# A decode attention block with its gradients: hand order on every engine, and weight-group transfers issued from GpSimd

## The chip, the cores and the metric

One core of a Trainium2 chip. The metric is device time in microseconds (us) of one execution, the median of the runs of a kernel. A "tile" is one head's K or V block, 128 partitions by 16 KB (2 MB).

## The reference

The forward pass of one decode step (layer norm, attention of one query over a cache of 8,192 positions in 32 heads, and a gated MLP in parallel) and the gradients of all its inputs except one constant:

```python
def _A_ref(x, k_cache, v_cache, wq, wo):       # Hq = Hkv = 32, Sk = 8192, Dh = 128, D = 640
    q = (x @ wq).reshape(B, Sq, Hq, Dh).transpose(0, 2, 1, 3)
    scores = jnp.einsum("bhqd,bhkd->bhqk", q, k) * (Dh ** -0.5)
    p = softmax(scores)
    o = jnp.einsum("bhqk,bhkd->bhqd", p, v)
    return o.transpose(0, 2, 1, 3).reshape(B, Sq, Hq * Dh) @ wo
def _B_ref(x, w1, w3, w2):                     # F = 1728
    return (silu(x @ w1) * (x @ w3)) @ w2
xn = layernorm(A_x)
out = A_x + _A_ref(xn, A_k_cache, A_v_cache, A_wq, A_wo) + _B_ref(xn, B_w1, B_w3, B_w2)
# returned: out, and its gradients for A_x, A_k_cache, A_v_cache, A_wq, A_wo, B_w1, B_w3, B_w2
```

The gradient of each K and V tile is an outer product as large as the tile. So the kernel reads about 152 MB and writes about 151 MB, and nearly all of it is 32 K and 32 V tiles in and 64 gradient tiles out.

## The kernel before

Ten tile slots hold K and V; a gradient overwrites its tile in place, is stored, and the slot takes the next load. All large transfers go through one in-order queue, SyncE's. Four heads form a group that shares a piece of `wq` and `wo`.

```python
    def fifo(out_, in_):
        tc.keep_in_program_order(nc.sync.dma_start(out_, in_))
    def load_group(g):                       # [cut: tile allocation]
        fifo(wq_g[:], wq_v[:, :, g * GW:(g + 1) * GW])
        fifo(wo_g[:], wo_v[:, g * GH:(g + 1) * GH, :])
    def load_next():
        if not pending or len(free_slots) < lag[0]:     # lag is 2 in the steady state
            return
        kind, h = pending.pop(0)
        if kind == "K" and h % GH == GH - 1 and h // GH + 1 < NG:
            load_group(h // GH + 1)
        t = free_slots.pop(0)
        fifo(t[:], (kc if kind == "K" else vc)[h])
    def store(kind, h):                      # [cut: bookkeeping]
        fifo((dkc if kind == "K" else dvc)[h], t[:])
        free_slots.append(t)
        load_next()
    # [cut]
    def finish_group(g):                     # [cut: small products]
        for hh in range(GH):
            nc.vector.tensor_scalar(wo_g[:, hh, :], g_bc[:], od[:, hh, 0:1], None, ALU.mult)
        fifo(dwo_v[:, g * GH:(g + 1) * GH, :], wo_g[:])
        for ci in range(NC):
            # [cut] wq_g becomes its gradient
        fifo(dwq_v[:, :, g * GW:(g + 1) * GW], wq_g[:])
    # [cut]
    for h in range(H):
        if hh == GH - 1 and g + 1 < NG:
            prep_group(g + 1)
        sums(h)                              # 64 + 64 matmuls: o and dq
        outer_v(h, 0, J // 2)
        outer_v(h, J // 2, J)
        store("V", h)
        if h == 1:
            mlp()
        if h + 1 < H:
            rows(h + 1)
            dots_k(h + 1)                    # transposes and products with q
        outer_k(h, 0, J // 2)
        if h + 1 < H:
            probs(h + 1)
        outer_k(h, J // 2, J)
        store("K", h)
        if h + 1 < H:
            dots_v(h + 1)
        if hh == GH - 1:
            finish_group(g)
```

A lag of 2 means that a load is issued only when two slots are on the free list. It goes into the slot freed one store earlier, so that it need not wait for the store that was issued just before it.

## Time and profile before

| | before |
|---|---|
| median time | 758.96 us (3 runs, 758.43 to 759.77) |
| bytes moved | 304.62 MB, mean 402 GB/s |
| TensorE busy | 79% |
| VectorE busy | 59% |
| ScalarE busy | 44% |

The largest wait of TensorE in the kernel before (us in total, times, longest us). No K or V load is among its waits anywhere in the list:

```profile
PE hb L352 <- DVE U L349: 41.0, 24, 2.7
```

The largest wait of SyncE's DMA queue in the same kernel is for stores to land:

```profile
SPq L99 <- DMA out_dram<-kv: 448.9, 55, 14.7
```

The timeline of TensorE around one head (start, us, operation, count, and the idle time before it) shows the hole that the change wants to fill, 1.67 us before the dq sums:

```profile
503.43 2.12 PE L347 MATMUL hb<-P,kv 128*128 128x64 bf16 x64
...
507.21 2.11 PE L352 MATMUL hb<-U,kv 128*128 128x64 bf16 x64 [1.67 <-DVE U L349]
```

The end of the kernel before, in a table of stretches of 4 us (stretch, length, busy time and count of PE, PEld, DVE, ACT, POOL, granted clock, DMA share, GB/s):

```profile
744.00:748.00 4.00, 0.00 (x0) 0.00 (x0) 0.00 (x0) 0.00 (x0) 0.00 (x0) 0.50 0.97 383
748.00:752.00 4.00, 0.00 (x0) 0.00 (x0) 0.00 (x0) 0.00 (x0) 0.00 (x0) 0.50 0.53 186
752.00:756.00 4.00, 0.00 (x0) 0.00 (x0) 0.00 (x0) 0.00 (x0) 0.00 (x0) 0.50 0.06 20
```

A share of 0.06 is 1/16: one packet in flight. The end is a drain of stores.

### The profile page before, as it was taken

The numbers are of one execution on the slowest core, as the hardware profiler recorded it, in microseconds if no ns is written. First come the engines' busy times: TensorE is split into PE (matmuls) and PEld (weight loads), VectorE is DVE, ScalarE is ACT, GpSimd is POOL, SyncE is SP. The second block draws the span as 40 slices with busy tenths as digits, with TensorE's granted clock in tenths as the row PEclk, the third lists the DMA queues.
The fourth block names the chain that finished last, engine by engine and source line by source line (L and its number), as shares of the span: only waits on it lengthen the run. The fifth ranks groups of instructions, "written<-read, shape, count | busy, mean of one in ns | idle before, by whom it ended". The sixth has DMA issues, their size and how long they took to land. (4 is left out here: it accounts for less than half of the span.)

```text
span 756.8 us, 25031 instructions
## 1 busy us (share of the span) xinstructions
PE 601.0 (79%) x11263; PEld 561.1 (74%) x11263; DVE 447.1 (59%) x771; ACT 330.7 (44%) x668; POOL 0.7 (0%) x6
## 2 busy tenths in 40 slices
PE   2988798888898888888898889888898889888820
PEld 2887688887788778877787778777787778777710
DVE  4369658654566557654666557654666557654470
ACT  1632354454454444444554445444554445444500
POOL 0000000000000000000000000000000000000000
PEclk9998999999998999999998999999998999999965
DMA  8999999999999999999999999999999999999996
GB/s 332 389 420 413 401 418 410 416 427 403 426 424 388 416 396 428 421 426 381 403 427 368 400 404 401 429 420 413 359 429 409 360 416 383 427 425 420 391 418 263
DMA packets 44031, 304.62 MB, mean 402 GB/s; under 512 B 2836, under 2 KB 24980, under 8 KB 27540
## 3 DMA queue, kind: packets, MB, share of 16 engines
q1 hardware_dynamic: 43616, 302.69, 98.3%
q8 instruction: 88, 1.44, 0.7%
q10 hardware_dynamic: 308, 0.33, 0.2%
q14 instruction: 19, 0.16, 0.1%
HBM read 151.67 MB, written 151.34 MB: 400 GB/s over the span
## 5 line engine op out<-in xcount | busy, mean ns | idle before, releaser
L269 ACT COPY KT<-pT 128x512 f32<-128x512 f32 x512 | 289.9, 588 | 120.7 <-PE pT L267 74.1
L267 PE MATMUL pT<-ident_f,kv 128*128 128x128 f32 x2048 | 317.5, 287 | 0.1
L267 PEld LDWEIGHTS pT<-ident_f,kv 128*128 128x128 f32 x2048 | 230.4, 147 | 0.5 <-ACT kv L483 0.4
L278 PEld LDWEIGHTS <-KT 128*128 128x128 bf16 x4096 | 176.6, 99 | 30.8 <-ACT KT L269 21.5
L328 DVE TENSOR_TENSOR kv<-qd,P 128x4096 bf16<-128x4096 bf16 x64 | 145.7, 2286 | 25.4 <-PE hb L347 25.4
L328 DVE TENSOR_TENSOR kv<-qd,U 128x4096 bf16<-128x4096 bf16 x64 | 143.6, 2284 | 0.0
L352 PE MATMUL hb<-U,kv 128*128 128x64 bf16 x2048 | 74.8, 199 | 42.1 <-DVE U L349 41.0
L352 PEld LDWEIGHTS <-kv 128*128 128x128 bf16 x2048 | 73.4, 102 | 45.3 <-issue 45.1
L278 PE MATMUL sA<-cz,KT 128*128 128x64 bf16 x2048 | 99.3, 193 | 7.2 <-ACT KT L269 6.5
L278 PE MATMUL dA<-cz,KT 128*128 128x64 bf16 x2048 | 99.3, 194 | 6.4 <-ACT KT L269 6.3
L343 DVE SCALAR_TENSOR_TENSOR U<-dA,P 128x64 bf16<-128x64 f32 x32 | 7.4, 230 | 132.6 <-PE dA L278 132.6
L354 ACT COPY od_g<-hb 128x2 f32<-128x2 f32 x32 | 5.1, 160 | 152.3 <-DVE kv L328 93.7
L347 PE MATMUL hb<-P,kv 128*128 128x64 bf16 x2048 | 67.7, 192 | 0.0
L347 PEld LDWEIGHTS <-kv 128*128 128x128 bf16 x2048 | 67.3, 98 | 0.0
L236 DVE SCALAR_TENSOR_TENSOR KT<-wo_g,g_bc 128x640 bf16<-128x640 bf16 x32 | 26.3, 823 | 28.5 <-PE dA L278 28.0
L308 PEld LDWEIGHTS sA<-rsum,pm_one 128*128 128x128 f32 x64 | 9.5, 187 | 29.0 <-ACT E L307 29.0
L308 PE MATMUL sA<-rsum,pm_one 128*128 128x1 f32 x64 | 12.2, 260 | 22.6 <-ACT E L307 22.1
L307 ACT ACTIVATE E<-sA,negM 128x64 f32<-128x64 f32 x32 | 10.1, 314 | 44.2 <-DVE negM L304 44.1
L292 ACT CAST qd<-pT 128x256 bf16<-128x256 f32 x32 | 12.1, 377 | 39.0 <-PE pT L289 39.0
L391 DVE SCALAR_TENSOR_TENSOR wq_g<-wq_g,KT 128x512 bf16<-128x512 bf16 x40 | 26.3, 687 | 3.7 <-ACT KT L382 3.7
L300 DVE TENSOR_REDUCE mrow<-sA 128x1 f32<-128x64 f32 x32 | 7.1, 222 | 35.8 <-PE sA L278 35.3
L315 DVE RECIPROCAL rZ<-sA 128x1 f32<-128x1 f32 x32 | 5.4, 169 | 30.9 <-PE sA L308 30.9
(119 smaller groups left out, 279.4 us busy)
## 6 DMA issues: line engine op xcount, KB each, us to landing
out_dram<-kv SPq DMA_DIRECT2D x64, 2048.0 KB, 21.2
kv<-in_A_k_cache_dram SPq DMA_DIRECT2D x32, 2048.0 KB, 15.7
kv<-in_A_v_cache_dram SPq DMA_DIRECT2D x32, 2048.0 KB, 17.6
wq_g<-in_A_wq_dram SPq DMA_DIRECT2D x8, 640.0 KB, 21.0
wo_g<-in_A_wo_dram SPq DMA_DIRECT2D x8, 640.0 KB, 22.6
out_dram<-wo_g SPq DMA_DIRECT2D x8, 640.0 KB, 16.3
out_dram<-wq_g SPq DMA_DIRECT2D x8, 640.0 KB, 17.4
kv<-in_B_w_dram SPq DMA_DIRECT2D x2, 1728.0 KB, 13.5
```

Of the source, the lines that this page charges most:

```text
L236: nc.vector.scalar_tensor_tensor(junk, wo_g[:, hh, :], 1.0, g_bc[:], ALU.mult, ALU.mult, accum_out=do_c[:, hh:hh + 1])
L267: nc.tensor.transpose(pT[:, k * P:(k + 1) * P], W3[:, 4 * c + k, :], ident_f[:])
L269: nc.scalar.copy(KT[:].rearrange("p k w -> p (k w)"), pT[:])
L278: nc.tensor.matmul(out_[:, 0:J], lhsT=KTb[:, k, par, :], rhs=cz[:, par, a, J - 2 - 2 * i:ZW - 2 * i], start=(i == 0 and par == 0), stop=(p ...
L292: nc.scalar.copy(qd[:].rearrange("p a d -> p (a d)"), ps_r[:, 0:2 * DH])
L307: nc.scalar.activation(E[:], sA[:, 0:J], ACTF.Exp, bias=negM[:], scale=1.0, accum_out=rsum[:])
L308: nc.tensor.matmul(sA[:, J + P:J + P + 1], lhsT=ones_b, rhs=rsum[:], start=False, stop=True, skip_group_check=True)
L328: nc.vector.tensor_tensor(dst[:, lo * DH:hi * DH].rearrange("p (j a b) -> p j a b", a=DH // 2, b=2), vec.rearrange("p (a b) -> p a b", b=2 ...
L343: nc.vector.scalar_tensor_tensor(U2[:, :, 0], dA[:, 0:J], 1.0, P2[:, :, 0], ALU.mult, ALU.mult, accum_out=rdot[:])
L347: nc.tensor.matmul(hb[:, 0:RW], lhsT=V3[:, j, :], rhs=P2[:, j, 0:1].to_broadcast([P, RW]), start=False, stop=(j == J - 1), skip_group_chec ...
L352: nc.tensor.matmul(hb[:, RW:2 * RW], lhsT=K3[:, j, :], rhs=U2[:, j, 0:1].to_broadcast([P, RW]), start=False, stop=(j == J - 1), skip_group ...
L391: nc.vector.scalar_tensor_tensor(wq_g[:, ci, :], wq_g[:, ci, :], 1.0, dqb, ALU.mult, ALU.mult, accum_out=dxa[:, ci, g:g + 1])
```

## The change

The intent: take TensorE's holes and the lump of group work out of each head. The scheduler is switched off, and each engine's instructions run in the order written. Transposes run on across head borders, softmax steps stand between outer products, group work is cut in pieces, and the group and MLP transfers leave SyncE's queue for GpSimd. Arithmetic and bytes stay, but for one small memset per head.

```diff
+    ctx.enter_context(tc.manual_schedule())
     def fifo(out_, in_):
-        tc.keep_in_program_order(nc.sync.dma_start(out_, in_))
+        nc.sync.dma_start(out_, in_)
-    def load_group(g):
+    def load_group(g, eng):
         wq_g = wpool.tile([P, NC, GW], BF16, name="wq_g", tag="wq_g")
-        fifo(wq_g[:], wq_v[:, :, g * GW:(g + 1) * GW])
+        eng.dma_start(wq_g[:], wq_v[:, :, g * GW:(g + 1) * GW])
# [cut: the same for wo_g]
         kind, h = pending.pop(0)
-        if kind == "K" and h % GH == GH - 1 and h // GH + 1 < NG:
-            load_group(h // GH + 1)
# [cut: prep_group, dots, sums, finish_group split in pieces of the same arithmetic]
+    def fin_wo(g):
+        G_ = grp[g]
         for hh in range(GH):
-            nc.vector.tensor_scalar(wo_g[:, hh, :], g_bc[:], od[:, hh, 0:1], None, ALU.mult)
-        fifo(dwo_v[:, g * GH:(g + 1) * GH, :], wo_g[:])
+            nc.vector.tensor_scalar(G_["wo"][:, hh, :], g_bc[:], G_["od"][:, hh, 0:1], None, ALU.mult)
+        nc.gpsimd.dma_start(dwo_v[:, g * GH:(g + 1) * GH, :], G_["wo"][:])
+    def fin_wq(g, ci):
# [cut]
+        if ci == NC - 1:
+            nc.gpsimd.dma_start(dwq_v[:, :, g * GW:(g + 1) * GW], wq_g[:])
+            grp.pop(g)
+            if g + 3 < NG:
+                load_group(g + 3, nc.gpsimd)
# [cut] in the MLP, five calls, seven transfers:
-            fifo(dv[:, 0:NA, :], wa)
+            nc.gpsimd.dma_start(dv[:, 0:NA, :], wa)
# [cut]
+    def head(h):
+        # [cut]
+        if has_prev:
+            outers_a(h - 1)              # outer products come one head later
+        side_k(h)                        # a piece of group work
+        for c in range(had, NCH):
+            T(h, "K", c)
+            if c >= 2:
+                M(h, "K", c - 2)
+        T(h, "V", 0)                     # V's transposes fill the softmax of K
+        M(h, "K", NCH - 2)
+        T(h, "V", 1)
+        M(h, "K", NCH - 1)
+        mx(h)
+        T(h, "V", 2)
+        mx_bc(h)
+        # [cut]
+        for c in range(2):
+            if c < pre:
+                T(h + 1, "K", c)         # the next head's K fills the end of V
+            M(h, "V", NCH - 2 + c)
+        rdot(h)
+        o_sum(h, 0, J // 2)              # the V sums lie round the correction of U
+        dsum(h)
+        o_sum(h, J // 2, J)
+        dq_sum(h)
```

## The prediction

> **What bounds the kernel now.** The page's DMA queue part gives the main queue 98.3% of 16 engines' span, but that overstates it. In the trace's packet records a 16 KB packet takes 611 ns at the median, 635 on average[...]. All packets at their size's median sum to 723 us per engine; they took 751, plus about 4 us of visible gaps: some 30 us of hidden starving. Stretches with a full queue run at 425 to 432 GB/s (windows table); after group boundaries they fall to 340 to 395.
>
> In the wait lists no engine waits for a K or V load in the whole run; SyncE waits for stores to land, and at times for compute. So compute sets the pace: in the timeline a head lasts 20.6 us (502.9 to 523.5), TensorE standing 3.5 of them: 1.7 before the dq sums (41 us in the run, for U), 0.8 before the sum of exponentials, the rest round the maximum and the dots. A group of four heads lasts 90.1 us (dwo issue to dwo issue): 7.7 us of group work in a lump. DMA work of a group: 16 tile transfers at 4.9 us plus 7.2 for wq, wo and their gradients (packets of 46 and 55 ns) is 85.4 us.
>
> **The change.** Arithmetic and bytes stay. One 0.17 us memset per head goes. Transposes of the next tile and of the next head's K fill the places where TensorE waited; the V sums are split round the U correction; group work comes in pieces of about 1 us; group and MLP outputs leave SyncE's in-order queue.
>
> TensorE per head: 16 chunks at 0.705 us (timeline) = 11.3, two sums at 2.1, 1.2 small products, about 1 of group work: 17 to 18. VectorE: 9.0 outer products, 1.8 small steps, 2.4 group pieces: 13. Compute then needs about 75 us per group, below DMA's 85.4. Bubbles and lump leave the critical path, but only 4.7 us per group (37 in all) can be cashed before DMA binds. Outer products come a head later, so tiles live longer; ten slots should cover that. At the MLP the pipeline drains; transfers queued by then last about until head 2 stores: a gap of 0 to 6 us.
>
> [...]
>
> **Estimate.** 270 MB of large packets at 427 GB/s = 632 us; small packets 94 us by their medians; start 2.6 and end 6 us as now; 2 us between span and time: 737. With a little for the MLP: **738 us**, 8 in 10 within **730 to 753**. Faster by over 2% (under 743.8): 0.70; within 2%: 0.27; slower: 0.03.
>
> **Signs.** TensorE now waits for loads of K or V; mean DMA 413 to 420 GB/s; the U wait falls from 41 us to a few; group period 85 to 87 us; excess packet time falls from 28 to about 10 us; TensorE busy share stays near 80%.
>
> **Wrong if:** GpSimd's descriptors slow the small packets or skew the engines; the MLP starves DMA longer than 6 us; VectorE's fixed order holds the maximum behind 6.8 us of outer products, so that compute stays near 21 us a head (then no waits for loads); or the full-queue rate falls when three queues mix.

Of the 16 KB packets of the kernel before, 504 took over 0.9 us (1.1 us at the median), 0.4% of those that started with fewer than two transfers of SyncE's queue not yet landed and 3.3% of the others.

## More of the kernel before

From the page of the kernel before: the span, the busy engines, the DMA total, and two of the queues (packets, megabytes, the time of their packets as a share of 16 engines' span).

```profile
span 756.8 us, 25031 instructions
...
PE 601.0 (79%) x11263; PEld 561.1 (74%) x11263; DVE 447.1 (59%) x771; ACT 330.7 (44%) x668; POOL 0.7 (0%) x6
...
DMA packets 44031, 304.62 MB, mean 402 GB/s; under 512 B 2836, under 2 KB 24980, under 8 KB 27540
...
q1 hardware_dynamic: 43616, 302.69, 98.3%
q8 instruction: 88, 1.44, 0.7%
```

Almost everything goes through q1. The last line looks negligible: 88 packets of 16 KB bring TensorE its instructions.

SyncE's issues in the kernel before, at the load of K of head 8 and of head 28, and the store of the `wo` gradient beside each (groups 0 and 5):

```profile
163.39 0.33 SPq L99 DMA_DIRECT2D kv<-in_A_k_cache_dram  x1
163.76 0.46 SPq L99 DMA_DIRECT2D out_dram<-wo_g  x1
...
612.81 0.33 SPq L99 DMA_DIRECT2D kv<-in_A_k_cache_dram  x1
613.18 0.76 SPq L99 DMA_DIRECT2D out_dram<-wo_g  x1
```

And VectorE's last operation on the `wo` gradient of the same two groups:

```profile
131.29 0.38 DVE L388 TENSOR_SCALAR wo_g<-g_bc,od_g 128x640 bf16<-128x640 bf16 x1
...
557.89 0.38 DVE L388 TENSOR_SCALAR wo_g<-g_bc,od_g 128x640 bf16<-128x640 bf16 x1
```

Compute needed (557.89 - 131.29)/5 = 85.3 us per group, but the queue needed (613.18 - 163.76)/5 = 89.9. The store was issued 32 us after its data were ready in group 0 and 55 us after in group 5: the queue fell behind by 4.6 us per group. Compute did not yet feel it, because it was living on the lead of the ten slots.

## The result and the profile after

| | before | after |
|---|---|---|
| median, us | 759.34 (4 runs, the three above and one more) | 753.03 (4 runs, 751.45 to 753.51) |
| ratio of fast runs | | 0.9915, 95% interval 0.9897 to 0.9933 |
| mean GB/s | 402 | 406 |
| TensorE busy, us | 601.0 | 593.0 |

Ratios here and below are the mean time of one kernel's fast runs over that of the other's of the same rounds, so not quite the ratio of the medians that are quoted. The change saves 6.3 us, 0.85%. The prediction was 738.

The page of the kernel after:

```profile
span 749.7 us, 25013 instructions
...
PE 593.0 (79%) x11263; PEld 565.3 (75%) x11263; DVE 447.7 (60%) x739; ACT 333.3 (44%) x668; POOL 30.4 (4%) x45
...
DMA packets 29136, 304.63 MB, mean 406 GB/s; under 512 B 2836, under 2 KB 5972, under 8 KB 12644
...
q1 hardware_dynamic: 22736, 276.39, 89.1%
q0 software_dynamic: 5984, 26.30, 8.7%
q8 instruction: 88, 1.44, 0.7%
```

The bytes are the same in 15,000 fewer packets; q0 is GpSimd's queue.

TensorE's waits after. It now waits for K and V loads (67.2 us together), and the wait for U has shrunk:

```profile
PE pT L274 <- DMA kv<-in_A_k_cache_dram: 60.1, 21, 5.4
...
PE hb L358 <- DVE U L365: 14.3, 32, 0.4
...
PE pT L274 <- DMA kv<-in_A_v_cache_dram: 7.1, 8, 1.5
```

SyncE's largest wait after, for stores to land, is longer by 133 us:

```profile
SPq L101 <- DMA out_dram<-kv: 581.6, 59, 18.4
```

TensorE's timeline after, at one head: the hole before the sums is down to 0.45 us, and a hole of 3.83 us has opened in front of a load instead.

```profile
318.19 0.63 PE L274 MATMUL pT<-ident_f,kv 128*128 128x128 f32 x4 [3.83 <-DMA kv<-in_A_k_cache_dram]
...
322.91 1.14 PE L358 MATMUL hb<-P,kv 128*128 128x64 bf16 x32 [0.45 <-DVE U L365]
```

SyncE's issues after: the stretch that follows the MLP, and then the K loads of heads 8 and 28.

```profile
116.70 0.33 SPq L101 DMA_DIRECT2D kv<-in_A_v_cache_dram  x1
130.49 0.33 SPq L101 DMA_DIRECT2D kv<-in_A_k_cache_dram  x1
130.87 1.19 SPq L101 DMA_DIRECT2D out_dram<-kv  x1
...
167.72 0.33 SPq L101 DMA_DIRECT2D kv<-in_A_k_cache_dram  x1
...
608.86 0.33 SPq L101 DMA_DIRECT2D kv<-in_A_k_cache_dram  x1
```

The stretches after the MLP, and the end, of the kernel after (columns as above):

```profile
120.00:130.00 10.00, 8.24 (x193) 7.76 (x193) 7.38 (x9) 2.79 (x6) 0.00 (x0) 1.00 0.81 340
130.00:140.00 10.00, 10.00 (x182) 9.78 (x181) 4.27 (x9) 7.80 (x16) 0.00 (x0) 1.00 0.87 298
...
736.00:740.00 4.00, 0.00 (x0) 0.00 (x0) 0.00 (x0) 0.00 (x0) 0.00 (x0) 0.50 0.87 371
740.00:744.00 4.00, 0.00 (x0) 0.00 (x0) 0.00 (x0) 0.00 (x0) 0.00 (x0) 0.50 0.28 119
744.00:748.00 4.00, 0.00 (x0) 0.00 (x0) 0.00 (x0) 0.00 (x0) 0.00 (x0) 0.50 0.06 25
```

Where the time went can be added up from the K load issues. From the load of head 8 to that of head 28 is five groups, in which the change saves 8.3 us: (612.81 - 163.39)/5 = 89.9 us per group before, (608.86 - 167.72)/5 = 88.2 after. The load of head 8 comes 4.3 us later, a loss at the MLP. From the load of head 28 to the end of the span it is 144.0 us before and 140.8 after, a gain of 3.1. In sum 7.1, the difference of the two profiled spans (756.8 and 749.7; the profiled run of the kernel after was its fastest).

So TensorE could go faster (it stands waiting for loads), and the transfers hardly do: 88.2 us per group, where the prediction had 85.4. The experiments ask why the transfers do not run faster, and which part of the change gave what.

### The profile page after: what moved, and what is told of

Its sections match the earlier page's. It is cut to its first block, busy times and chain, and to the rows that moved or that the text cites. A ratio compares the mean times of both kernels' runs of the same rounds, so it can differ in the third digit from the quotient of the medians.

```text
span 749.7 us, 25013 instructions
## 1 busy us (share of the span) xinstructions
PE 593.0 (79%) x11263; PEld 565.3 (75%) x11263; DVE 447.7 (60%) x739; ACT 333.3 (44%) x668; POOL 30.4 (4%) x45
## 4 chain that ended last, share of the span: by engine, by line
DMA 59%; PE 27%; DVE 8%; issue 2%; ACT 1%; SPq 1%; ACTq 0%; DVEq 0%
DMA out_dram<-kv 39%; DMA kv<-in_A_k_cache_dram 15%; PE pT L274 11%; DMA kv<-in_A_v_cache_dram 4%; PE hb L358 4%; DVE kv L379 3%; PE dA L293 3%; PE sA L293 3%; PE hb L373 3%; DVE U L365 1%; PE dh_ps L462 1%; PE acc L536 1%; PE gu_ps L451 1%; PE sA L320 1%; DVE kv L539 0%
## 5 line engine op out<-in xcount | busy, mean ns | idle before, releaser
L274 PE MATMUL pT<-ident_f,kv 128*128 128x128 f32 x2048 | 335.2, 288 | 67.8 <-DMA kv<-in_A_k_cache_dram 60.1
L276 ACT COPY KT<-pT 128x512 f32<-128x512 f32 x512 | 299.3, 586 | 183.8 <-PE pT L274 151.1
L274 PEld LDWEIGHTS pT<-ident_f,kv 128*128 128x128 f32 x2048 | 223.5, 145 | 72.2 <-issue 68.7
L293 PEld LDWEIGHTS <-KT 128*128 128x128 bf16 x4096 | 196.0, 100 | 19.9 <-issue 12.8
L293 PE MATMUL dA<-cz,KT 128*128 128x64 bf16 x2048 | 106.6, 196 | 8.8 <-ACT qd L310 6.6
L358 PE MATMUL hb<-P,kv 128*128 128x64 bf16 x2048 | 81.6, 201 | 14.3 <-DVE U L365 14.3
L365 DVE SCALAR_TENSOR_TENSOR U<-dA,hb,P 128x128 bf16<-128x128 f32 x32 | 11.4, 355 | 35.3 <-PE hb L363 35.3
L429 DVE SCALAR_TENSOR_TENSOR wq_g<-wq_g,side 128x512 bf16<-128x512 bf16 x40 | 27.3, 682 | 0.0
L233 DVE SCALAR_TENSOR_TENSOR side<-wo_g,g_bc 128x640 bf16<-128x640 bf16 x32 | 26.2, 817 | 0.3
L323 DVE TENSOR_REDUCE negM<-sA 128x1 f32<-128x128 f32 x32 | 9.3, 291 | 18.6 <-PE sA L320 18.6
```

What stands on the lines that cost most here:

```text
L233: nc.vector.scalar_tensor_tensor(junk[:], G_["wo"][:, hh, :], 1.0, g_bc[:], ALU.mult, ALU.mult, accum_out=G_["do"][:, hh:hh + 1])
L274: nc.tensor.transpose(pT[:, k * P:(k + 1) * P], W3[:, 4 * c + k, :], ident_f[:])
L276: nc.scalar.copy(KT[:].rearrange("p k w -> p (k w)"), pT[:])
L293: nc.tensor.matmul(S_[kind][:, 0:J], lhsT=KTb[:, k, par, :], rhs=S_["cz"][:, o:o + J], start=(i == 0 and par == 0), stop=(par == 1), skip_ ...
L323: nc.vector.tensor_reduce(S_["negM"][:], S_["K"][:, J:J + P], AX.X, ALU.max, negate=True)
L358: nc.tensor.matmul(S_["hb"][:, 0:RW], lhsT=V3[:, j, :], rhs=S_["P2"][:, j, 0:1].to_broadcast([P, RW]), start=(j == 0), stop=(j == J - 1), ...
```

## The experiments

All ratios are to the kernel before in the same rounds on the same chip (its medians were 758.8 to 759.5 us). A result is correct unless "wrong" is written. Sums of packet times are worked out from the trace's packet records, per engine (the sum of all, divided by 16). "Excess" is the time of the 16 KB packets above 611 ns each, their median in the kernels before and after. The runs were made on several chips (e1 to e4 on one; e5, e6, e7 and e9 on a second; e8, e10, e11 and e12 on a third; e13 to e16 on a fourth), so differences of medians between rounds are uncertain by about 1 us; the ratios, which are to the same round, give the same picture wherever both are quoted.

| run | edit in words | us | ratio (95%) |
|---|---|---|---|
| e1_after_lag3 | after, lag 3 | 748.96 | 0.9864 (0.9844 to 0.9885) |
| e2_before_group_pool | before, group transfers on GpSimd | 750.05 | 0.9879 (0.9862 to 0.9896) |
| e3_hand_all_on_sp | hand order, all transfers on SyncE | 752.55 | 0.9904 (0.9887 to 0.9920) |
| e4_after_mlp_on_sp | after, MLP outputs on SyncE | 748.89 | 0.9862 (0.9845 to 0.9879) |
| e5_after_mlp_sp_lag3 | e4 and lag 3 | 749.08 | 0.9869 (0.9857 to 0.9882) |
| e6_before_lag3 | before, lag 3 | 760.55 | 1.0032 (1.0012 to 1.0052) |
| e9_stores_on_pool | after, K/V stores on GpSimd too | 750.56 | 0.9890 (0.9877 to 0.9903) |
| e7_dma_only_lag2 | e4's transfers, no arithmetic | 720.10 | 0.9486 (0.9474 to 0.9498) |
| e8_dma_pe_many | e7 and 11,250 idle matmuls | 740.77 | 0.9767 (0.9747 to 0.9787) |
| e13_dma_pe_half | e7 and 5,625 idle matmuls | 728.40 | 0.9590 (0.9577 to 0.9603) |
| e10_dma_pe_few | e7 and 780 long idle matmuls | 721.38 | 0.9510 (0.9491 to 0.9529) |
| e11_e4_split | e4, 8 loads cut in two | 782.84 (two of the six runs slow) | 1.0298 (1.0271 to 1.0326) |
| e12_e2_split | e2, 8 loads cut in two | 778.54 | 1.0261 (1.0241 to 1.0281) |
| e14_e4_more_small | e4 and 2,048 idle small matmuls | 753.84 | 0.9928 (0.9915 to 0.9940) |
| e15_e4_more_large | e4 and 288 idle large matmuls | 750.71 | 0.9887 (0.9871 to 0.9903) |
| e16_e4_fewer | e4, half the sums' matmuls | 744.25 | 0.9800 (0.9785 to 0.9815) |

Not every expectation was met: e1 landed between its two theories, e6 came 0.6 us over its range, e8 1.2 and e13 0.6 us under theirs, e15 0.7 over its own, and e9, e11 and e12 did not give what was hoped for. The theories and the "if" branches of the expectations are guesses made before the run; what each outcome says is told below.

### Taking the change apart: e2, e3, e4

First theory: the transfers are held back where the queue's packets starve, because loads wait for a store that has just been issued; and the MLP's outputs on GpSimd cost the gap seen at 120 to 140 us. Rival: the GpSimd queue itself is what slows the transfers.

e2 is the kernel before, with only the group transfers moved:

```diff
+    def fifo_p(out_, in_):
+        tc.keep_in_program_order(nc.gpsimd.dma_start(out_, in_))
     def load_group(g):
+        fifo = fifo_p if g > 0 else fifo_sp
# [cut]
-        fifo(dwo_v[:, g * GH:(g + 1) * GH, :], wo_g[:])
+        fifo_p(dwo_v[:, g * GH:(g + 1) * GH, :], wo_g[:])
# [cut: dwq_v likewise]
```

> The kernel before, automatic schedule, with only the transfers of wq, wo and their gradients (groups 1 to 7 and all gradients) issued from GpSimd; MLP transfers stay on SyncE. Theory C (all of the gain is the transfers: GpSimd packs 1,024 and 1,280 byte rows into packets of 4,096 and 5,120 bytes, and no small transfer blocks SyncE's queue): about 749 to 752, as fast as the whole change or faster. Theory D (the gain is the hand order, compute set the pace before): about 757 to 760.

e3 is the hand order alone, with group and MLP transfers back on SyncE and the group loads at their former place:

```diff
         kind, h = pending.pop(0)
+        if kind == "K" and h % GH == GH - 1 and h // GH + 1 < NG:
+            load_group(h // GH + 1, nc.sync)
# [cut]
-        nc.gpsimd.dma_start(dwo_v[:, g * GH:(g + 1) * GH, :], G_["wo"][:])
+        nc.sync.dma_start(dwo_v[:, g * GH:(g + 1) * GH, :], G_["wo"][:])
# [cut: dwq_v and the five MLP calls likewise; later group loads removed]
```

> The changed kernel, hand order kept, with all group and MLP transfers back on SyncE's queue, group loads at the places of the kernel before. Theory C: the gain is lost, 756 to 762. Theory D: most of it stays, 750 to 754, and waits of TensorE on K and V loads show in both cases.

e4 puts only the MLP outputs back:

```diff
-            nc.gpsimd.dma_start(dv[:, 0:NA, :], wa)
+            nc.sync.dma_start(dv[:, 0:NA, :], wa)
# [cut: the other four calls likewise]
```

> The changed kernel with only the five MLP output transfers back on SyncE. In the changed kernel GpSimd's store of the w3 gradient, issued at 90.3 us, landed only at about 130 us, where a load waited for it and held the ready store of head 2 behind it; from 127 to 131 us no packet of the main queue ran. If that blocking costs what the gap shows, 4 to 5 us come back: about 748 to 749, and the stretch of 120 to 140 us moves at 400 GB/s or more. If not, 753.

With the MLP outputs on SyncE in all four, this is a full square of the other two parts:

| | groups on SyncE | groups on GpSimd |
|---|---|---|
| automatic order | 759 (before) | 750.05 (e2) |
| hand order | 752.55 (e3) | 748.89 (e4) |

Either part alone gains 9 or 6 us, and both together about 10, not 15. They meet a common floor near 749. The loads of K show the same: from head 8 to head 28 one group takes 89.9 us before, but 88.1 in e2, 88.6 in e3, 88.4 in e4. A faster TensorE is not what is worth most here: e2 leaves the order of the arithmetic alone and gains more than e3. Why e3 gains 6 us at all, with compute not the limit, no run separates.

What e2 gains from is partly visible in the packets: from GpSimd the group transfers go out in packets of 4,096 and 5,120 bytes (159 and 198 ns at the median) where SyncE used 1,024 and 1,280 (46 and 55 ns). All packets but the 16 KB ones sum to 102.5 us per engine before and 97.9 in e2. A second queue raised no rate (the fastest of the page's 40 slices moved 429 GB/s before, with none of these transfers on GpSimd, and 428 after), but these transfers still cost less from there. Only a part of e2's 9 us is explained so (4.6 us); the rest, presumably the group transfers no longer standing in the in-order queue, was not separated.

The change as it stands loses 4 us of this again: 753.03 against e4's 748.89. The stretches of e4 after the MLP, to be held against 0.81 and 0.87 above:

```profile
120.00:130.00 10.00, 8.18 (x191) 7.67 (x189) 7.38 (x9) 2.87 (x6) 0.00 (x0) 1.00 1.02 381
130.00:140.00 10.00, 10.00 (x184) 9.79 (x182) 4.18 (x8) 7.85 (x16) 0.00 (x0) 1.00 1.01 427
```

In the kernel after, GpSimd issues the store of the `w3` gradient at 90.25 us, and SyncE's next load, which needs that slot, comes out only at 130.49:

```profile
90.25 0.76 POOL L540 DMA_DIRECT2D out_dram<-kv  x1 [5.98 <-DVE kv L539]
```

The V store that stands behind this load in the in-order queue was ready near 112 us and goes out at 130.87. So the engines run short while work lies ready. The GpSimd store landed 40.2 us after its issue (its 16 completion packets end from 120.79 to 130.43 us), where the stores of this size that SyncE issued in the kernel before took 17.1 us at the median. Why it takes so long is inferred, not shown. In the packet records the two queues get about as many packets as each other while both have work: from 90 to 100 us 201 packets of 5,120 bytes of GpSimd's queue start beside 195 of 16 KB of SyncE's, and from 120 to 127 us 122 of 6,912 bytes beside 126 (from 110 to 120 us it is 268 beside 141). So the queue with the smaller packets moves fewer bytes. At the end of e5, from 735.6 to 740.2 us, packets of GpSimd's queue (160 ns) and of SyncE's (614 ns) follow one another in turn.

### Is it the slow packets? e1, e5, e6, e9

The packet records of the kernel after still have 18.7 us per engine of excess in the 16 KB packets. With a lag of 3 a load never waits for a store issued shortly before. If the slow packets were the cost, this should return most of it.

```diff
-    lag[0] = 2
+    lag[0] = 3
```

> The changed kernel with one number changed: a load goes into a slot only when three slots are free, not two, so the store whose landing SyncE awaits before that load was issued one store earlier. Theory A (the 16 DMA engines run at different points, a store lands only when the slowest is done, and SyncE, in order, puts too little behind it, so that fast engines run dry and restart slowly): the excess of 16 KB packets over 611 ns falls from 18.7 us to under 10 and the time from 753 to about 740. Theory B (slow packets come from memory whatever the queue depth, loads and stores meeting): 753, within 3 us, excess unchanged. Either way some 4 us at 127 to 131 us may stay, or go if the store of head 2 is no longer blocked.

> The changed kernel with MLP outputs on SyncE and loads at three free slots, the two edits that each gave 4 us alone. If they remove different losses: about 745. If there is a common floor of the transfers near 748: 748 to 749.

> The kernel before with only the number of free slots that a load waits for raised from two to three. If the waits for landings cost it as they cost the changed kernel (4 us came back there): 753 to 755. If its compute pace sets its time, as the prediction said: 757 to 760.

The excess fell from 18.7 to 10.9 us in e1, and all packets now sum to 732.9 us per engine instead of 740.5. Yet the time fell by only 4 us, to the same 749; and e4, which stands at 749 with a lag of 2, gained nothing from a lag of 3 (e5). In the kernel before, a lag of 3 costs 0.3%. So e1 fits neither of its theories. The end of e5 shows where the rest went (columns as above):

```profile
728.00:732.00 4.00, 0.93 (x3) 0.59 (x3) 1.12 (x5) 0.00 (x0) 0.15 (x1) 0.50 0.66 256
732.00:736.00 4.00, 0.00 (x0) 0.00 (x0) 0.00 (x0) 0.00 (x0) 0.00 (x0) 0.50 0.06 26
736.00:740.00 4.00, 0.00 (x0) 0.00 (x0) 0.00 (x0) 0.00 (x0) 0.00 (x0) 0.50 0.06 26
740.00:744.00 4.00, 0.00 (x0) 0.00 (x0) 0.00 (x0) 0.00 (x0) 0.00 (x0) 0.50 0.07 29
```

For 12 us about one packet is in flight at a time. The other engines are done and one carries on with its share. So the slow packets and the starving look like a symptom. Every transfer of SyncE's queue ends in 16 small completion packets, as many as there are engines (the records of e4 have 2,304 for 144 transfers), and SyncE waits for the last of them: after the GpSimd store above, whose 16 are spread over 9.6 us, its wait ends 22 ns after the last. My reading is that with the short lag all engines wait for the late one as they go, and that with the longer lag it falls behind and finishes alone; no run tests this reading by itself. The theory that starving sets the time, which was also the prediction's, fell here.

e9 asked whether the order of stores and loads in one queue was the limit, by moving the K and V stores to GpSimd too (and later group loads one head back):

```diff
-        fifo((dkc if kind == "K" else dvc)[h], t[:])
+        nc.gpsimd.dma_start((dkc if kind == "K" else dvc)[h], t[:])
```

> The changed kernel with the stores of the K and V gradients issued from GpSimd too (and the loads of later groups one head later, so that GpSimd does not wait for the landing of a gradient), so that SyncE's queue holds loads alone and a load waiting for a landing no longer holds back a store that is ready. If the in-order queue is what starves the DMA engines: no gap at 127 to 131 us, excess of 16 KB packets under 12 us, time 740 to 745. If stores written by software are slower, or loads and stores interleaved packet by packet meet in memory: 750 or more.

750.56: the same floor again, although the excess fell to 6.9 us and the stretch of 120 to 130 us ran at 417 GB/s, as the first branch wanted. The order of one queue is not what makes the floor.

### What makes one engine late: e7, e8, e13, e10

New theory: something that only the computing kernel does loads the DMA engines unevenly, and the candidate on the page is q8, TensorE's instruction packets. Rivals: the GpSimd queue burdens some engines; or the transfers alone have this floor.

e7 keeps e4's transfers, in the same queues and with lag 2, and drops the arithmetic (wrong):

```diff
-    for h in range(H):
-        # [cut: head(h), outers, MLP, group work]
+    for h in range(H):
+        if h == 2:
+            mlp_dma()
+        store("V", h)
+        store("K", h)
+        if h % GH == GH - 1:
+            group_out(h // GH)
```

> Wrong results on purpose: the changed kernel without any of its arithmetic. The same loads, stores, slots and waits of SyncE's queue (a load when two slots are free), group transfers from GpSimd, MLP outputs on SyncE, each tile stored as it was loaded. If the compute of the changed kernel still sets its time, this runs at 735 or less. If the transfers and the waits between them are the whole of it, it takes 744 to 750, like the changed kernel with MLP outputs on SyncE (748.9), with slow packets still there (excess of the 16 KB packets 15 us or more).

720.1 us, 29 below the floor. The last stretches of e7 (columns as above) show hardly a late engine: the share falls from full to 0.40 and 0.01 without standing at 0.06 (in the packet records the last engine ends 1.7 us after the one before it).

```profile
708.00:712.00 4.00, 0.00 (x0) 0.00 (x0) 0.00 (x0) 0.00 (x0) 0.00 (x0) 1.00 1.02 438
712.00:716.00 4.00, 0.00 (x0) 0.00 (x0) 0.00 (x0) 0.00 (x0) 0.00 (x0) 1.00 0.40 170
716.00:720.00 4.00, 0.00 (x0) 0.00 (x0) 0.00 (x0) 0.00 (x0) 0.00 (x0) 1.00 0.01 4
```

The GpSimd transfers are all in it (19.66 MB on its page), and the kernel before, which has none, ends with a share of 0.06 all the same, so they are not the burden. (This is not quite the computing kernel's stream: without compute, group transfers run ahead.) What is missing is the compute and its instructions. By the letter of the expectation this was the branch "compute still sets its time"; it does not tell waiting for results from the load that the instructions themselves put on the DMA engines. The next three runs do.

e8 adds matmuls that share no data and no waits with the transfers, as many as the kernel has; e13 half as many; e10 few long ones that keep TensorE just as busy (all wrong):

```diff
+    pe_out = pst()
+    for _ in range(11250):                   # e13: 5625
+        nc.tensor.matmul(pe_out[:, 0:P], lhsT=ident_bf[:], rhs=ident_bf[:], start=True, stop=True)
# e10 instead:
+    for _ in range(780):
+        nc.tensor.matmul(pe_out[:], lhsT=ident_f[:], rhs=pe_in[:], start=True, stop=True)   # 512 columns, f32
```

> Wrong results on purpose: the transfers-only kernel (720.1 us) plus 11,250 small matmuls on TensorE that touch nothing the transfers touch (constant operands). That is as many TensorE instructions as the real kernel has, so the trace should hold 88 instruction packets of 16 KB again. Theory F (the instruction fetch goes through one of the 16 DMA engines, which then also carries its sixteenth of the data; stores land only when that engine is done, so it sets the time): 742 to 750, one engine alone in flight at the end or the others slowed. Theory G (the transfers are slowed by compute writing and reading SBUF tiles, or by late stores): 720 to 723.

> Wrong results on purpose: the transfers-only kernel plus 780 large matmuls (512 columns, 4-byte operands), so TensorE is busy about as long as with the 11,250 small ones but fetches hardly any instructions. Theory F: 720 to 722, as without TensorE work. If TensorE being busy slows transfers by itself (power, SBUF reads): clearly more, 730 or above.

> Wrong results on purpose: transfers only plus 5,625 small matmuls, half the dose (44 instruction packets instead of 88). Theory F (each instruction packet delays the one DMA engine that fetches it): half of the way from 720.1 to 740.8, so 729 to 732. If the cost is not proportional to the fetches: 720 to 724 or 738 and above.

From the page of e8:

```profile
span 738.7 us, 22846 instructions
...
PE 630.7 (85%) x11260; PEld 630.4 (85%) x11260; DVE 5.1 (1%) x24; ACT 1.6 (0%) x2; POOL 25.1 (3%) x36
...
q8 instruction: 88, 1.44, 0.7%
```

From the page of e10, TensorE busier still, with 12 packets:

```profile
PE 672.7 (93%) x1570; PEld 297.7 (41%) x1570; DVE 5.6 (1%) x25; ACT 1.6 (0%) x2; POOL 25.1 (3%) x36
...
q8 instruction: 12, 0.20, 0.1%
```

| run | instruction packets | us over e7 | per packet |
|---|---|---|---|
| e10 | 12 | 1.3 | 0.11 |
| e13 | 44 | 8.3 | 0.19 |
| e8 | 88 | 20.7 | 0.24 |

From the ratios the three costs are 1.8, 7.9 and 21.3 us; that of e10 is within the noise.

The cost goes with the instructions and not with TensorE's busy time. It is not quite proportional: half the packets cost 40% in e13. The 16 KB packets themselves tell the same: per engine they sum to 627.6 us in e7, 628.6 in e10, 630.6 in e13 and 639.6 in e8. 20.7 us is four times what the page's 0.7% suggests: 0.7% of the span, spread over 16 engines, would be 5 us each. One more thing differs between e8 and e10, what TensorE reads from SBUF; from the shapes and the page's counts I estimate that e10 reads about 0.7 of what e8 does (two matmuls, so 1,560, for the 780 written, with 320 KB of operands each, against 11,250 with 64 KB each), and it costs a sixteenth. So that is hardly the cause.

That these packets carry TensorE's instructions is read from their number. With 2 x 11,263 = 22,526 instructions of TensorE on the page (it counts a weight load for each matmul) there are 88 packets of 16 KB, 256 instructions for each; e10 has 3,140 and 12, 262 for each; e7, with 20, has none of this queue on its page. In a kernel that its transfers bound, what these packets cost shows in the transfers (20.7 us in e8).

### Is it one engine, and which? e11, e12

If the fetch loads one engine, giving that engine less data should cure it. Eight K loads were cut into 120 and 8 partitions, so that one engine would be spared. Which engines the two parts go to is assumption, as are "the last one", "the lowest 8" and "between" in the expectation below: no trace shows it (the records name no engine).

```diff
+        if kind == "K" and h % 4 == 2:
+            fifo(t[0:120, :], kc[h][0:120, :])
+            fifo(t[120:P, :], kc[h][120:P, :])
+        else:
             fifo(t[:], (kc if kind == "K" else vc)[h])
```

> The changed kernel with MLP outputs on SyncE (748.9), in which 8 of the 64 tile loads are cut into 120 and 8 partitions. [...] Theory F, if the engine with the instruction fetch is the last one: 726 to 736. If it is among the lowest 8: 750 to 756. If it is between, or theory G: within 2 us of 749.

> The kernel before with group transfers from GpSimd (750.05), with the same 8 loads cut. If the cut relieves the limiting engine in the hand-ordered kernel, this tells what the hand order is worth once the transfers no longer hide it: with compute at 90.1 us a group as in the kernel before, its time stays at 743 to 750 while the hand-ordered one falls to 726 to 736. If both fall alike, compute is not the limit in either.

Both failed as tests. e11 took 33 us more than e4 (its four fast runs: 779.5 to 784.9 us), e12 28 us more than e2: the cut transfers themselves are slow. Around most of them the rate stays under 290 GB/s for 2 to 10 us, at the lowest 203 to 221. About 4 us were lost for each of the eight. The small completion packets went from 2,304 to 2,360: 7 more for each cut load, so 23 for its two parts where a whole load has 16. Whether one engine was spared is not shown, and the slow rate hides whatever the relief may have brought.

The packet records answer the first half of the question after all, although they name no engine. Where the queue is full, 16 packets are under way most of the time (in 83% of samples from 140 to 690 us of the kernel before and 88% after), which I take as one for each engine, and a next packet starts a few ns before one ends (mostly 14 to 16 ns after a fetch in these two kernels). So from a packet one can step back along its engine, as long as only one predecessor fits. In e8 just 16 packets are under way in the middle of 73 of the 88 fetches, the fetch included: it takes a turn of one engine, 0.95 us at the median. For 69 of the 88, a slow 16 KB packet (over 0.7 us) starts as the fetch ends, and takes 1.07 us at the median in place of 0.61. Now step back from each fetch. Over all runs the engine could be followed past the time of the fetch before in 354 cases (33 of them in e8), and that fetch was never on it. In the four cases where the path reached an earlier fetch (one in e8, two in e13, one in e14), it was the eighth before. **So the fetches do not sit on one engine, as Theory F had it; from these four cases I estimate that they go round eight.** If so, each of the eight engines spends 14 to 15 us on its 11 fetches in e8 (0.95 us for each, and about 0.46 for the slow packet after most), most of the 20.7 us. The one engine that ends late is then not explained by the fetches alone: the last engine ends 4.2 us after the one before it in e8, 4.9 in e4. Why, and which engine it is, stays open.

### In the real kernel: e14, e15, e16

e16 has the same transfers as e4 and 2,048 matmuls fewer (both sums over every second column, wrong); e14 has 2,048 small idle matmuls more; e15 has 288 large idle ones, a control with e14's TensorE time and few instructions.

```diff
# e16, in both sums:
-        for j in range(J):
+        for j in range(0, J, 2):
# e14, after dq_sum(h) of each head:
+        for _ in range(64):
+            nc.tensor.matmul(px[:, 0:64], lhsT=ident_bf[:], rhs=ident_bf[:, 0:64], start=True, stop=True)
# e15, there:
+        for _ in range(9):
+            nc.tensor.matmul(px[:], lhsT=ident_bf[:], rhs=g_bc[:, 0:512], start=True, stop=True)
```

> The changed kernel with MLP outputs on SyncE (748.9) plus 64 idle matmuls of 64 columns at the end of each head, 2,048 in all: 16 more instruction packets, about 1.9 us more TensorE time per head, which the hand order has to spare (it waits 65 us for loads). Theory F: 16 packets at 0.24 us (20.7 us over 88) is 4 us: 752 to 754.

> The control: the same kernel plus 9 idle matmuls of 512 columns per head, about the same 1.9 us of TensorE time in 288 instructions more, 2 packets. Theory F: 748.5 to 750. If TensorE time is what counts, the same as with the 2,048 small ones.

> Wrong results on purpose: the changed kernel with MLP outputs on SyncE, in which both sums over the 64 columns take only every second one: 2,048 matmuls and 16 instruction packets fewer. Theory F: 744 to 746. If the fetch does not limit it, 748 to 750, since TensorE was waiting for loads already.

| run | instruction packets | us | against e4 | TensorE busy, us |
|---|---|---|---|---|
| e16 | 72 | 744.25 | -4.6 | 564.0 |
| e4 | 88 | 748.89 | | 595.1 |
| e15 | 90 | 750.71 | +1.8 | 638.6 |
| e14 | 104 | 753.84 | +4.9 | 632.2 |

e4 was run on another chip; from the ratios the differences are -4.7, +1.9 and +5.0 us. e16 is the cleanest one. TensorE's waits in e4, and then in e16:

```profile
PE pT L274 <- DMA kv<-in_A_k_cache_dram: 58.2, 20, 5.4
...
PE pT L274 <- DMA kv<-in_A_v_cache_dram: 6.4, 7, 1.5
```

```profile
PE pT L274 <- DMA kv<-in_A_k_cache_dram: 72.3, 24, 5.3
PE pT L274 <- DMA kv<-in_A_v_cache_dram: 25.8, 14, 3.8
```

In e4 these two waits sum to 64.6 us, so TensorE already had time to spare; in e16 they sum to 98.1. TensorE's 31 us less of work went into waiting, and yet the time fell by 4.6 us, 0.29 us for each of the 16 packets that are gone. e14 rose by 4.9 us, but it is not clean: there TensorE's waits for loads are down to 5.4 us, so that its longer work may itself have begun to count. e15, with slightly more TensorE time, rose by 1.8; it still waits 28.2 us for loads. The difference of 3.1 us between the two fits 14 packets at 0.22 us. Some of e16's gain may be TensorE time too: if all of e15's 1.8 us came from its 43.5 us more of it, 31 us less would be worth 1.3 us, which leaves 3.3 us or more for the 16 packets, 0.21 us each.

## Why the prediction was wrong

The time was 753.03 us where 738 was predicted, a hair over the range of 730 to 753, and within 2% of before, to which the prediction gave 0.27. The mechanism on TensorE was right; what bounds the kernel was not. Point by point:

1. **"So compute sets the pace ... A group of four heads lasts 90.1 us (dwo issue to dwo issue)": wrong, a misread marker.** That issue is SyncE's and stands in an in-order queue. VectorE finished a group every 85.3 us; the queue took 89.9. The prediction set 90.1 for compute against 85.4 for DMA, and the two were about the reverse. That no engine waits for a load showed a lead of ten slots being used up, 4.6 us per group, not that compute was the limit. Of "37 in all" to be cashed nothing was there as compute time. What the hand order does gain alone is 6 us (e3), and why is not shown.

2. **"270 MB of large packets at 427 GB/s = 632 us": the mis-sized term, by 12 us.** The 16 KB packets summed to 644.4 us per engine in the kernel after. What was left out is TensorE's instruction fetch: with the transfers alone that sum is 627.6 us (e7), idle matmuls raise it to 639.6 (e8) and the time by 20.7 us, and in the real kernel e16 gives 0.21 to 0.29 us of time per packet. And the term took the mean of 16 engines, which is not the bound either: e1 lowered all packets' sum by 7.6 us and the time by only 4, leaving some 12 us at the end with about one packet in flight. Per group the sum comes out near: 85.4 predicted, and 11 packets at 0.24 us give 2.6, so 88.0, where the loads of K measured 88.2 after and 88.4 in e4.

3. **"excess packet time falls from 28 to about 10 us": wrong.** It went from 27.9 to 24.2 (all sizes). When e1 did push it down, the time fell by only 4 us, and in e5 not at all.

4. **TensorE's holes: right in kind, worth little.** The U wait fell from 41.0 to 14.3 us ("a few" was predicted) and TensorE came to wait for loads, 67.2 us, as predicted. Holes filled on an engine that is not the limit turn into other holes.

5. **Mean rate "413 to 420 GB/s": wrong**, 402 to 406. **Group period "85 to 87": slightly missed**, 88.2 by the K loads.

6. **MLP gap "0 to 6 us": right in size, by luck.** It cost 4 us (e4), by stores on GpSimd that hold a slot back; the prediction's reason, the drained pipeline, was not the one.

7. **GpSimd's queue:** the fastest of the page's 40 slices moved 429 GB/s before and 428 after, and larger packets made its transfers cheaper: packets other than the 16 KB ones summed to 96.1 us after against 102.5 before, against the 94 of the estimate.

What stays open: why one engine ends late, and which; why an engine's packet after a fetch is slow; the 8 us between e8 (740.8) and the floor of the real kernel (748.9), where stores also have to wait for compute; the exact split of e2's gain; and where e3's gain comes from.

The best version is e4, or e1 within its error: 748.9 us, 4 us below the kernel after and 10 below the kernel before. The one edit that went below it with the compute in place has fewer TensorE instructions (e16, wrong); no change of order or queue tried here did.

## What to carry to other kernels

Take the pace of compute from the compute engines' own events and the pace of transfers from the queue's, over several periods: an issue in an in-order queue tells when its turn came, not when its data were ready, and a growing lag between the two (32 us in group 0, 55 in group 5 here) says who is falling behind. In a kernel near the transfer limit, look at the engine that finishes last and not only at the mean of 16; a tail of the run with a share of 1/16 betrays it (12 us in e5). Count instruction packets as load on the DMA engines: with some 22,000 TensorE instructions they cost 20.7 us in e8, more than all the holes that were filled (6 us in e3).
